# Products of softmax weights and values, per head in halves of TensorE's columns, in a kernel of block-sparse attention and a gated feed-forward block

## The chip, the cores and the metric

The kernel runs on one core of a Trainium2 chip. The metric is device time in microseconds (us): the median of three runs, 801.23 before the change (798.42 to 802.46). The engines of the core work side by side, each with its own queue of instructions: TensorE (PE; its weight loads are shown as PEld), VectorE (DVE), ScalarE (ACT), GpSimd (POOL), and SyncE (SP), which only issues DMAs.

## The reference

Four batches, eight heads of 64, 768 positions in 24 blocks of 32. A block of queries attends to itself and its two neighbours, to the first and last block, and to three sampled blocks; the first and last block attend to everything. A gated feed-forward block follows.

```python
scores = scale * np.matmul(q, k.transpose(0, 1, 3, 2))
mask = np.abs(blk_i - blk_j) <= window
mask = mask | (blk_i == 0) | (blk_j == 0) | (blk_i == n_blocks - 1) | (blk_j == n_blocks - 1)
...
scores = np.where(mask, scores, -1000000000.0)
scores = scores - np.max(scores, axis=-1, keepdims=True)
attn = np.exp(scores)
attn = attn / (np.sum(attn, axis=-1, keepdims=True) + 1e-09)
return np.matmul(attn, v).astype(np.float32)
...
g = x @ w_gate
silu = g * (1.0 / (1.0 + np.exp(-g)))
val = x @ w_val
return (silu * val @ w_out).astype(np.float32)
```

## The kernel before

**Numbers in two parts.** In batches 1 to 3 and in most of the feed-forward part an f32 number is held as two f16 numbers, high and low, and a product of two such numbers is three f16 products: high with high, high with low, low with high. Batch 0's attention is computed in f32 by functions of its own (`pair0`, `full_rows0`).

**Chunks.** The queries of each batch are taken in groups of 128 (four blocks); the chunks that the feed-forward part works on have two such groups in batch 0 (three chunks) and three in batches 1 to 3 (six chunks). For each chunk attention writes the tile `xall`, and then come 24 pieces of the first feed-forward product (`p`, L1693, 12 matmuls of 384 columns each) and 12 pieces of the second (`po`, L1756, 9 matmuls of 512 columns each). A chunk's feed-forward part begins when all of its attention is written; the norm `xn` (L1637) is part of that beginning.

**One block of queries, batches 1 to 3 (`block`).** VectorE copies the keys of the eight visible blocks into a ring of three slots (`kring`, L1114 and L1115), and DMAs bring the values to a ring of three (`w2all`: window by SyncE, L1121, the sampled blocks by GpSimd's indirect DMA, L1124). Two blocks form a pair: their scores (`qk`, L1137) are one task on PE of 32 matmuls, each in a quarter of PE's columns. Then VectorE takes the maxima (L1151), ScalarE the exponentials (L1168), the weights are split into high (ScalarE, L391) and low (VectorE, L394), and SyncE issues a transposing DMA that puts keys on the partitions (`pts`, L1193). Then comes the product with the values (`pv`, L1206): for each of four pairs of heads 6 matmuls of 64 columns, all 128 rows and 128 columns of PE wide. Both heads' values are the stationary operand (128 columns) and both heads' weights the moving one (64 columns), so that half of what is computed, one head's values with the other head's weights, isn't used. When two blocks have their products, `x_high` (ScalarE, L1227) and `x_low` (VectorE, L1232) write the high and the low part to `xall`, each with one instruction for each half of the partitions, because the two heads of a pair lie in different columns.

The rows of the first and the last block (`full_rows`) have scores `qkf` (L922) and products `pvf` (L991) in halves of PE's columns: one head's output in partitions 0 to 63, the other's in 64 to 127. Their products already hold the high and the low weights side by side as one moving operand.

**What sets the order.** The whole program is a list of tasks, each with an engine, a planned duration, the tasks that it needs, the ring buffers that it takes, and a rank. `Plan.order` runs through planned time. Whenever an engine is free, it takes the task of lowest rank among those that are ready and have their buffers. Ranks are a base (10 for each chunk of attention, 1000 more for its feed-forward part) plus an entry of the table `SHIFT`, which reaches from about -8700 to 6200. A task becomes ready 0.16 us (`SEM_US`) after the last task that it needs has ended. `in_turn` makes each task of a kind need the one before it of that kind; products of blocks and of full rows are of one kind, `"pv"`, scores of both are of one kind, `"qk"`. The pieces of the feed-forward part need each other in the same way. The order in which each engine's instructions are then issued is this planned order; on the chip every engine keeps to it.

The loads of a batch's keys and values (`load_kv`) go through SyncE's queue, in order with the transposing DMAs of attention.

Of the kernel before, what the change touches and what calls it, by code (L numbers as in the profile page):

```python
# [18 lines left out]
BLK = 32  # L19
# [22 lines left out]
DMA_US = 1.6  # L42
SEM_US = 0.16
# [61 lines left out]
class Task:  # L105
    __slots__ = ("eng", "us", "emit", "need", "rank", "take", "dma", "left", "outs", "next", "ready", "end", "no", "key", "late", "many")
# [13 lines left out]
class Plan:  # L120
# [9 lines left out]
    def add(self, eng, us, emit, need=(), rank=0.0, take=(), use=(), dma=None, behind=None, late=0.0, many=1):  # L130
        t = Task()
        t.late, t.many = late, many if dma is not None and eng != "POOL" else 0
# [31 lines left out]
    def order(self):  # L164
# [9 lines left out]
        done = []  # L174
        now = 0.0
        while len(done) < len(self.tasks):
            later = []
            moved = False
            for eng, list_ in waiting.items():
# [4 lines left out]
                for t in list_:  # L184
                    if t.ready > now:
                        later.append(t.ready)
                        continue
                    if best is not None and (t.rank, t.no) > (best.rank, best.no):
                        continue
# [8 lines left out]
                    best = t  # L198
# [6 lines left out]
                free[eng] = now + t.us  # L205
                t.end = now + t.us + t.late
                if t.dma is not None:
                    queue = max(max(queue, now + min(0.4, t.us)) + t.dma, t.end)
                    t.end = queue + DMA_US
                    for _ in range(t.many):  # L210
                        lanes.append(max(lanes.pop(0), t.end))
# [16 lines left out]
def tile_block_sparse_attn_swiglu(  # L228
# [657 lines left out]
    def full_rows(b, ci, sub, o, rank):  # L886
# [23 lines left out]
        for j in range(4):  # L910
# [43 lines left out]
            s = in_turn("qk", "PE", 0.87, scores, [o.done] + bt.k_done, rank, take=qk, use=[o.qs, bt.ks])  # L954
# [27 lines left out]
            def product(j=j, turned=turned):  # L982
                if j == 0:
                    get(pv, f"pvf_{b}")
                for c6 in range(6):
# [3 lines left out]
                    for l, w in ((0, P), (1, D)):  # L989
                        for hh in range(2):  # L990
# [8 lines left out]
            pvs.append(in_turn("pv", "PE", 0.68, product, there + vl, rank, take=[] if j else [pv],  # L999
                               use=turned + vbuf + ([pv] if j else [])))  # L1000
# [50 lines left out]
    def attention(ci, rank, qtiles):  # L1051
        b = CHUNKS[ci][0] // NTB
        bt = batches[b]
        for sub, si in enumerate(CHUNKS[ci]):
# [27 lines left out]
            for n in range(0, len(sparse), 2):  # L1082
                r = r0 + 0.05 * n
                if not b:
# [4 lines left out]
                       for i in range(2)]  # L1089
                first = [next(x) for x in two]  # L1090
                qks = [x[2] for x in first]
                a = in_turn("qk", "PE", 1.0, lambda first=first: [x[1]() for x in first], [x[0] for x in first] + [o.done], r,
                            take=qks, use=[o.qs])
# [4 lines left out]
    def block(ci, b, bt, o, sub, n, qb, col, rank, tsc, pv):  # L1098
# [96 lines left out]
        def product():  # L1195
# [3 lines left out]
            pvv = pv.tile.rearrange("p (j b q) -> p j b q", j=4, b=2)  # L1199

            for j in range(4):
                g, u = divmod(2 * j, 4)
                i = 0
                for cc in range(2):
                    for l, m in ((0, 0), (0, 1), (1, 0)):
                        nc.tensor.matmul(  # L1206
                            pvv[:, j, n % 2],
                            vg[:, cc, l, 2 * j : 2 * j + 2, :],
                            pq[:, g, m, cc, u : u + 2, :],
                            start=i == 0,  # L1210
                            stop=i == 5,
                        )
                        i += 1
# [3 lines left out]
        def x_views(hh):  # L1217
            hs_ = slice(hh * D, (hh + 1) * D)
            pvv = pv.tile.rearrange("p (j b q) -> p j b q", j=4, b=2)
            src = pvv[hs_, :, :, hh * BLK : (hh + 1) * BLK]  # L1220
            xt = xts[ci].tile
            return [src] + [xt[hs_, l, :, cols].rearrange("p j (b q) -> p j b q", b=2) for l in range(2)]

        def x_high():
            for hh in range(2):
                src, hi, _ = x_views(hh)
                nc.scalar.copy(hi, src)  # L1227

        def x_low():
            for hh in range(2):  # L1230
                src, hi, lo = x_views(hh)
                nc.vector.tensor_tensor(lo, src, hi, op=ALU.subtract)  # L1232
# [14 lines left out]
        a = in_turn("pv", "PE", 0.71, product, [a, vl, vi], rank, take=[pv] if n % 2 == 0 else [], use=[pts] + ([pv] if n % 2 else []))  # L1247
# [607 lines left out]
```

## Time and profile before

| | |
|---|---|
| median of three runs | 801.23 us (798.42 to 802.46) |
| the profiled execution | 800.0 us |
| its span, first to last instruction | 798.2 us |
| granted TensorE clock, mean of the span | 0.989 |
| products `pv`, L1206 | 1584 matmuls, busy 57.0 us |
| scores `qk`, L1137 | 1056 matmuls, busy 35.7 us |
| feed-forward `p`, L1693 | 2016 matmuls, busy 326.8 us |
| feed-forward `po`, L1756 | 900 matmuls, busy 195.3 us |

All of this is of one profiled execution. The views used below are: the page's busy times; busy time of each engine by stretches of the span; PE's timeline, in which consecutive matmuls of one line are one row with its start, its length from the first start to the last modelled end, and their count; groups of instructions by line and shape (after the bars: busy us, mean ns of one, and idle time before them); and waits. Matmuls overlap, so that rows of PE's timeline do too: the time that a group takes is read from its start to the next group's start.

### The profile page before, as it was taken

What the parts mean: (1) busy time and instruction counts of PE and PEld (TensorE: products, weight loads), DVE (VectorE), ACT (ScalarE), POOL (GpSimd) and SP (SyncE); (2) the same over time, 40 slices, a digit from 0 to 9 for tenths busy, and PEclk for the clock granted to TensorE, in tenths of its full rate; (3) what the DMA queues carried; (4) which work ended last, traced back from release to release, by engine and by line L of the source; (5) the groups of instructions that cost most, each with busy time, mean ns of one, the idle gap of its engine ahead of it and who ended that gap; (6) DMA issues with size and microseconds to landing.
All of it is one profiled execution on the core that took longest, in us unless ns stands there. A gap on an engine that the chain in (4) does not pass through costs nothing.

```text
span 798.2 us, 21196 instructions
## 1 busy us (share of the span) xinstructions
PE 762.4 (96%) x8098; PEld 489.2 (61%) x8098; DVE 547.4 (69%) x1658; ACT 504.5 (63%) x1211; POOL 205.7 (26%) x257
## 2 busy tenths in 40 slices
PE   3789999999999999999999999999999999999998
PEld 2557778884587566645665566645665566555655
DVE  5676898998898787742799866753798767731220
ACT  2687767587688686763598856754487757641221
POOL 3553511322033223201223222401223233101210
PEclk9889999999999999999999999999999999999999
DMA  8963537647877979478769994947878974330001
GB/s 205 259 220 118 193 146 260 205 125 230 198 151 172 212 169 197 91 197 265 159 134 182 269 227 114 203 97 211 188 133 179 228 177 105 69 69 19 1 1 39
DMA packets 171430, 128.08 MB, mean 160 GB/s; under 512 B 115008, under 2 KB 136896, under 8 KB 171328
## 3 DMA queue, kind: packets, MB, share of 16 engines
q1 hardware_dynamic: 165696, 109.42, 56.6%
q0 software_dynamic: 5632, 17.31, 8.5%
q8 instruction: 63, 1.03, 0.5%
q14 instruction: 39, 0.32, 0.1%
HBM read 79.50 MB, written 11.01 MB: 113 GB/s over the span
## 4 chain that ended last, share of the span: by engine, by line
PE 63%; DVE 18%; DMA 8%; issue 4%; ACT 4%; SPq 1%; DVEq 1%; ACTq 0%
PE p L1693 29%; PE po L1756 18%; PE pv L1206 4%; PE p L1687 3%; DMA q<-in_q_dram 3%; PE qk L1137 3%; DVE pp L394 2%; DVE act L1702 1%; DVE act L1707 1%; DMA pts<-pp 1%; DVE w1t L394 1%; DVE e L1151 1%; DMA stage<-in_k_dram 1%; DVE kring L1114 1%; PE qk L1341 1%
## 5 line engine op out<-in xcount | busy, mean ns | idle before, releaser
L1693 PE MATMUL p<-xall,w1t 128*128 128x384 f16 (+1 forms) x2016 | 326.8, 319 | 0.0
L1693 PEld LDWEIGHTS <-w1t 128*128 128x128 f16 x2016 | 191.2, 98 | 115.5 <-issue 8.5
L1715 POOL TENSOR_TENSOR h<-act,h 128x384 f16<-128x384 f32 (+1 forms) x108 | 101.6, 941 | 372.5 <-ACT h L1712 372.1
L1756 PE MATMUL po<-w2all,h 128*128 128x512 f16 (+1 forms) x900 | 195.3, 371 | 0.3 <-DVE w2all L394 0.3
L1756 PEld LDWEIGHTS <-h 128*128 128x128 f16 x900 | 84.6, 98 | 93.7 <-issue 5.6
L1712 ACT CAST h<-act 128x384 f16<-128x384 f32 (+1 forms) x108 | 50.8, 471 | 82.5 <-DVE act L1707 82.2
L1124 POOL DMA_INDIRECT w2all<-vd,vidx x66 | 62.8, 951 | 150.2 <-PE pv L1206 126.7
L1702 DVE SCALAR_TENSOR_TENSOR act<-act,p 128x384 f32<-128x384 f32 (+1 forms) x108 | 54.2, 504 | 65.2 <-ACT act L1698 64.5
L1687 PE MATMUL p<-xall,w1t 128*128 128x256 f32 x384 | 88.8, 384 | 0.4 <-DVE act L1702 0.3
L1168 ACT ACTIVATE e<-e,nb,es 128x256 f32<-128x256 f32 x132 | 78.2, 593 | 2.2
L1687 PEld LDWEIGHTS p<-xall,w1t 128*128 128x128 f32 x384 | 71.4, 192 | 12.0 <-DVE w2all L394 1.4
L1698 ACT ACTIVATE act<-p,gsc 128x384 f32<-128x384 f32 (+1 forms) x84 | 47.0, 560 | 31.2 <-PE p L1693 30.6
L1707 DVE SCALAR_TENSOR_TENSOR act<-act,hs,p 128x384 f32<-128x384 f32 (+1 forms) x84 | 49.7, 591 | 21.8 <-PE p L1693 18.8
L1206 PEld LDWEIGHTS <-w2all 128*128 128x128 f16 x1584 | 55.1, 98 | 13.9 <-issue 3.8
L394 DVE SCALAR_TENSOR_TENSOR pp<-e,rr,pp 128x256 f16<-128x256 f32 x132 | 61.2, 510 | 1.3 <-ACT pp L391 1.0
L391 ACT ACTIVATE pp<-e,rr 128x256 f16<-128x256 f32 x132 | 58.1, 496 | 3.7 <-DVE rr L782 2.5
L1206 PE MATMUL pv<-pts,w2all 128*128 128x64 f16 x1584 | 57.0, 193 | 2.8 <-DMA pts<-pp 2.8
L1151 DVE CUSTOM_DVE_ANT_1 e<-qk,msk 128x256 f32<-128x256 f32 x132 | 50.0, 417 | 2.8 <-issue 2.4
L1593 ACT ACTIVATE ot<-po,oc 128x512 f32<-128x512 f32 (+1 forms) x25 | 16.7, 667 | 42.9 <-PE po L1756 42.7
L1114 DVE COPY kring<-kst 128x256 f16 x198 | 38.9, 251 | 5.6 <-PE qk L1137 5.3
L1232 DVE TENSOR_TENSOR xall<-pv,xall 64x256 f16<-64x256 f32 x66 | 27.7, 420 | 21.1 <-ACT xall L1227 18.7
L1137 PE MATMUL qk<-kring,qs 128*32 128x256 f16 x1056 | 35.7, 274 | 0.2 <-DVE mx L1151 0.2
(187 smaller groups left out, 899.4 us busy)
## 6 DMA issues: line engine op xcount, KB each, us to landing
stage<-in_w_dram SPq DMA_DIRECT2D x36, 512.0 KB
w2all<-vd SPq DMA_DIRECT2D x66, 192.0 KB
qs<-qraw SPq DMA_DIRECT2D x72, 128.0 KB
out_dram<-ot SPq DMA_DIRECT2D x19, 256.0 KB
qn<-in_q_dram SPq DMA_DIRECT2D x36, 128.0 KB
qraw<-in_q_dram SPq DMA_DIRECT2D x36, 128.0 KB
stage<-in_v_dram SPq DMA_DIRECT2D x9, 512.0 KB
vd<-stage SPq DMA_DIRECT2D x9, 512.0 KB
```

What stands on the lines that cost most here:

```text
L391: nc.scalar.activation(hi, src, AF.Copy, scale=scale)
L394: nc.vector.scalar_tensor_tensor(lo, src, scale, hi, op0=ALU.mult, op1=ALU.subtract)
L1124: nc.gpsimd.indirect_dma_start(vf[0:96, 1, :], None, bt.vd, bass.IndirectOffsetOnAxis(ap=vidx[0:96, qb : qb + 1], axis=0))
L1137: nc.tensor.matmul(stv[u * BLK : (u + 1) * BLK, g].rearrange("p s k -> p (s k)"), o.q[:, l, h // 2, h % 2, col : col + BLK], kg[:, h].rear ...
L1151: nc.vector.tensor_tensor_reduce(ev[:, g], stv[:, g], o.g.msk[:, qb, :].unsqueeze(2).broadcast_to([P, 8, BLK]), scale=1.0, scalar=-3.0e38, ...
L1168: nc.scalar.activation(ev[:, g], ev[:, g], AF.Exp, bias=nb_[:, g : g + 1], scale=o.g.es[:, 0:1], accum_out=c["rs"][:, g : g + 1],)
L1206: nc.tensor.matmul(pvv[:, j, n % 2], vg[:, cc, l, 2 * j : 2 * j + 2, :], pq[:, g, m, cc, u : u + 2, :], start=i == 0, stop=i == 5,)
L1687: nc.tensor.matmul(t[:, 0:tc_], w[:, i + 1, k_ * P : (k_ + 1) * P], x_k(k_), start=k_ == 0, stop=k_ == NKT - 1)
L1693: nc.tensor.matmul(t[:, 0:tc_], w_[:, f, m, k_, :], x_k(k_, l), start=i == 0, stop=i == 11)
L1702: nc.vector.scalar_tensor_tensor(a_, a_, 1.0, pg.tile[:, 0:tc_], op0=ALU.add, op1=ALU.mult)
L1715: nc.gpsimd.tensor_tensor(hv(f)[:, 1, :], act.tile[:, 0:tc_], hv(f)[:, 0, :], op=ALU.subtract)
L1756: nc.tensor.matmul(po.tile[:, cs], hv(f)[:, l, ts_], w2h[:, f, m, cs], start=f == 0 and i == 0, stop=f == NF - 1 and i == 2)
```

## The change

The product of a block is made per head. The head's values are the stationary operand (64 columns), the output goes to its own half of the partitions, so that PE works in halves of its columns, and the two heads of a pair alternate. The head's high values meet its high and low weights side by side as one moving operand of 64 columns (high in the first 32, low in the second); its low values meet the high weights, 32 columns, added to the first half. So there are 32 matmuls for a block instead of 24. In the output the two halves of 64 columns must now be added: `x_high` rounds the first half to the high part, one instruction over all partitions, and `x_low` subtracts that from the first half and then adds the second half, two instructions over all partitions.

The planner gets a mark `thin` for the tasks in which PE works in parts of its columns (scores and products of blocks and of full rows in batches 1 to 3), a price of 0.097 us for PE's change between such tasks and others, and a rule: after a thin task, PE takes a ready thin task before any other, whatever the ranks. (`HOLD_US` holds only for tasks marked 2, of which there is none.) The planned durations of the thin tasks and of `x_high` and `x_low` are new. The table `SHIFT` stays as it is.

```diff
+TURN_US = 0.097
+HOLD_US = 6.0
...
-    def add(self, eng, us, emit, need=(), rank=0.0, take=(), use=(), dma=None, behind=None, late=0.0, many=1):
+    def add(self, eng, us, emit, need=(), rank=0.0, take=(), use=(), dma=None, behind=None, late=0.0, many=1, thin=False):
         t = Task()
+        t.thin = thin
...
+        thin = False
...
-                    if t.ready > now:
-                        later.append(t.ready)
+                    at = t.ready + (HOLD_US if t.thin == 2 and not thin else 0.0)
+                    if at > now:
+                        later.append(at)
                         continue
-                    if best is not None and (t.rank, t.no) > (best.rank, best.no):
+                    key = (eng == "PE" and thin and not t.thin, t.rank, t.no)
+                    if best is not None and key > low:
                         continue
...
-                    best = t
+                    best, low = t, key
...
-                free[eng] = now + t.us
-                t.end = now + t.us + t.late
+                us = t.us
+                if eng == "PE":
+                    us += TURN_US if bool(t.thin) != thin else 0.0
+                    thin = bool(t.thin)
+                free[eng] = now + us
+                t.end = now + us + t.late
...
-            s = in_turn("qk", "PE", 0.87, scores, [o.done] + bt.k_done, rank, take=qk, use=[o.qs, bt.ks])
+            s = in_turn("qk", "PE", 0.66, scores, [o.done] + bt.k_done, rank, take=qk, use=[o.qs, bt.ks], thin=True)
...
-            pvs.append(in_turn("pv", "PE", 0.68, product, there + vl, rank, take=[] if j else [pv],
-                               use=turned + vbuf + ([pv] if j else [])))
+            pvs.append(in_turn("pv", "PE", 0.54, product, there + vl, rank, take=[] if j else [pv],
+                               use=turned + vbuf + ([pv] if j else []), thin=True))
...
-                a = in_turn("qk", "PE", 1.0, lambda first=first: [x[1]() for x in first], [x[0] for x in first] + [o.done], r,
-                            take=qks, use=[o.qs])
+                a = in_turn("qk", "PE", 0.87, lambda first=first: [x[1]() for x in first], [x[0] for x in first] + [o.done], r,
+                            take=qks, use=[o.qs], thin=True)
...
-            pvv = pv.tile.rearrange("p (j b q) -> p j b q", j=4, b=2)
+            out_ = pv.tile.rearrange("p (j b lq) -> p j b lq", j=4, b=2)
 
             for j in range(4):
-                g, u = divmod(2 * j, 4)
-                i = 0
                 for cc in range(2):
-                    for l, m in ((0, 0), (0, 1), (1, 0)):
-                        nc.tensor.matmul(
-                            pvv[:, j, n % 2],
-                            vg[:, cc, l, 2 * j : 2 * j + 2, :],
-                            pq[:, g, m, cc, u : u + 2, :],
-                            start=i == 0,
-                            stop=i == 5,
-                        )
-                        i += 1
+                    for l, w in ((0, 2), (1, 1)):
+                        for hh in range(2):
+                            g, u = divmod(2 * j + hh, 4)
+                            nc.tensor.matmul(
+                                out_[hh * D : (hh + 1) * D, j, n % 2, 0 : w * BLK],
+                                vg[:, cc, l, 2 * j + hh, :],
+                                pq[:, g, 0:w, cc, u, :],
+                                start=cc == 0 and l == 0,
+                                stop=cc == 1 and l == 1,
+                            )
...
-        def x_views(hh):
-            hs_ = slice(hh * D, (hh + 1) * D)
-            pvv = pv.tile.rearrange("p (j b q) -> p j b q", j=4, b=2)
-            src = pvv[hs_, :, :, hh * BLK : (hh + 1) * BLK]
+        def x_views():
+            pvv = pv.tile.rearrange("p (j b l q) -> p j b l q", j=4, b=2, l=2)
             xt = xts[ci].tile
-            return [src] + [xt[hs_, l, :, cols].rearrange("p j (b q) -> p j b q", b=2) for l in range(2)]
+            return [pvv[:, :, :, i, :] for i in range(2)] + [xt[:, l, :, cols].rearrange("p j (b q) -> p j b q", b=2) for l in range(2)]
 
         def x_high():
-            for hh in range(2):
-                src, hi, _ = x_views(hh)
-                nc.scalar.copy(hi, src)
+            src, _, hi, _ = x_views()
+            nc.scalar.copy(hi, src)
 
         def x_low():
-            for hh in range(2):
-                src, hi, lo = x_views(hh)
-                nc.vector.tensor_tensor(lo, src, hi, op=ALU.subtract)
+            src, more, hi, lo = x_views()
+            nc.vector.tensor_tensor(lo, src, hi, op=ALU.subtract)
+            nc.vector.tensor_tensor(lo, more, lo, op=ALU.add)
...
-        a = in_turn("pv", "PE", 0.71, product, [a, vl, vi], rank, take=[pv] if n % 2 == 0 else [], use=[pts] + ([pv] if n % 2 else []))
+        a = in_turn("pv", "PE", 0.47, product, [a, vl, vi], rank, take=[pv] if n % 2 == 0 else [], use=[pts] + ([pv] if n % 2 else []), thin=True)
...
-            a = add("ACT", 0.76, x_high, [a, x_open(ci, rank)], rank, use=[pv, xts[ci]])
-            x_done[ci].append(add("DVE", 0.87, x_low, [a], rank, use=[pv, xts[ci]]))
+            a = add("ACT", 0.42, x_high, [a, x_open(ci, rank)], rank, use=[pv, xts[ci]])
+            x_done[ci].append(add("DVE", 0.88, x_low, [a], rank, use=[pv, xts[ci]]))
```

More of the change, by code (lines that the diff above doesn't have):

```diff
@@ L105 @@
 class Task:
-    __slots__ = ("eng", "us", "emit", "need", "rank", "take", "dma", "left", "outs", "next", "ready", "end", "no", "key", "late", "many")
+    __slots__ = ("eng", "us", "emit", "need", "rank", "take", "dma", "left", "outs", "next", "ready", "end", "no", "key", "late", "many", "thin")
 class Buf:
@@ L204, in order @@
                     self.given[b.ring].append(b)
-                free[eng] = now + t.us
-                t.end = now + t.us + t.late
+                us = t.us
[4 more added lines that the diff above has]
+                t.end = now + us + t.late
                 if t.dma is not None:
-                    queue = max(max(queue, now + min(0.4, t.us)) + t.dma, t.end)
+                    queue = max(max(queue, now + min(0.4, us)) + t.dma, t.end)
                     t.end = queue + DMA_US
```

## The prediction

> **What bounds the kernel now.** I read the page first: engine shares.
>
> ```profile
> span 798.2 us, 21196 instructions
> PE 762.4 (96%) x8098; PEld 489.2 (61%) x8098; DVE 547.4 (69%) x1658; ACT 504.5 (63%) x1211; POOL 205.7 (26%) x257
> ```
>
> TensorE (PE) is busy for 96% of the span. An average hides stages, so the second view is the busy time by stretches, cut at the places where the feed-forward part of a chunk begins (460, 547, 636) and where attention ends (712). Columns after the stretch: its length, then busy time of PE, weight loads, VectorE (DVE), ScalarE (ACT), GpSimd (POOL), granted clock, DMA share, GB/s.
>
> ```profile
> core 0: us, PE busy (x) PEld busy (x) DVE busy (x) ACT busy (x) POOL busy (x), PEclk, DMA share, GB/s
> 0.00:205.00 205.00, 177.54 (x2230) 133.21 (x2231) 164.93 (x382) 141.95 (x329) 69.21 (x110) 0.96 0.66 196
> 205.00:396.00 191.00, 187.69 (x1973) 120.10 (x1971) 136.58 (x461) 129.68 (x313) 45.31 (x51) 1.00 0.78 181
> 396.00:460.00 64.00, 63.23 (x792) 38.01 (x791) 57.03 (x220) 54.59 (x143) 18.46 (x19) 1.00 0.88 194
> 460.00:547.00 87.00, 87.00 (x864) 51.00 (x862) 51.40 (x160) 50.68 (x126) 20.65 (x22) 1.00 0.76 168
> 547.00:636.00 89.00, 87.95 (x937) 52.80 (x939) 69.06 (x245) 62.60 (x156) 23.04 (x24) 1.00 0.82 181
> 636.00:712.00 76.00, 76.00 (x819) 45.91 (x808) 52.19 (x162) 45.95 (x116) 18.01 (x19) 1.00 0.54 117
> 712.00:798.00 86.00, 83.00 (x507) 48.16 (x503) 16.23 (x33) 19.03 (x33) 10.96 (x12) 1.00 0.05 16
> ```
>
> The change works in batches 1 to 3, whose attention lies between 205 and 712 us. PE idles there for 3.31 + 0.77 + 0 + 1.05 + 0 = 5.1 us of 507. Up to 205 nothing changes (batch 0 has products of its own), and from 712 on only feed-forward work is left. So a microsecond less of PE work between 205 and 712 is a microsecond of time, but only while PE has other work to go on with. In 396 to 460 VectorE is busy for 57.03 of 64 us and DMA is at 0.88: there attention has limits of its own. That decides the case, so I looked at the borders of the chunks, in the timeline of PE (start, length, line, operation, count).
>
> ```profile
> 455.66 4.06 PE L1756 MATMUL po<-w2all,h 128*128 128x512 f16 x18
> 459.56 0.81 PE L1637 MATMUL xn<-sqx,ones_h 128*128 128x384 bf16 x4
> ...
> 543.25 4.05 PE L1756 MATMUL po<-w2all,h 128*128 128x512 f16 x18
> 547.13 2.11 PE L1693 MATMUL p<-xall,w1t 128*128 128x384 f16 x12
> ...
> 635.44 1.06 PE L1137 MATMUL qk<-kring,qs 128*32 128x256 f16 x32
> 636.43 2.12 PE L1693 MATMUL p<-xall,w1t 128*128 128x384 f16 x12
> ```
>
> At 459.56, 547.13 and 636.43 the last output products (po) of a chunk are followed at once by the first work of the next (xn or p), which needs that chunk's finished attention. At these three places PE has no stock of feed-forward work left.
>
> **The product itself.** The timeline of PE in a dense stretch:
>
> ```profile
> 432.65 2.11 PE L1756 MATMUL po<-w2all,h 128*128 128x512 f16 x9
> 434.69 1.06 PE L1137 MATMUL qk<-kring,qs 128*32 128x256 f16 x32
> 435.68 2.12 PE L1756 MATMUL po<-w2all,h 128*128 128x512 f16 x9
> ...
> 440.27 0.86 PE L1206 MATMUL pv<-pts,w2all 128*128 128x64 f16 x24
> 440.98 2.11 PE L1756 MATMUL po<-w2all,h 128*128 128x512 f16 x9
> 442.92 0.86 PE L1206 MATMUL pv<-pts,w2all 128*128 128x64 f16 x24
> ...
> 445.56 0.86 PE L1206 MATMUL pv<-pts,w2all 128*128 128x64 f16 x24
> ...
> 448.30 1.06 PE L1137 MATMUL qk<-kring,qs 128*32 128x256 f16 x32
> ```
>
> Lengths overlap, so I go from start to start. Nine full-width po matmuls of 512 columns take 442.92 - 440.98 = 1.94 us, 0.421 ns a column. The old product (pv, 24 matmuls) takes 440.98 - 440.27 = 0.70 us, 29 ns each, of which 27 are its 64 columns. The scores (qk) work in quarters of the array's columns. The po before them takes 434.69 - 432.65 = 2.04, so 0.10 goes on entering the narrow form. The scores then take 0.99, of which 8 rounds x 256 columns x 0.421 = 0.86 are streaming, so 0.13 goes on leaving it, small starts included. Narrow work that stands alone pays 0.23.
>
> For halves of the columns there is a near relative, the product of the full rows (pvf): 6 rounds of two pairs, one of 128 and one of 64 columns.
>
> ```profile
> 327.27 0.71 PE L991 MATMUL pvf<-ptsf,stage 128*64 128x128 f16 x24
> 327.91 2.12 PE L1693 MATMUL p<-xall,w1t 128*128 128x384 f16 x12
> ```
>
> It takes 0.64. Two halves one after the other would stream 2304 columns, 0.97 us; side by side 1152, 0.49. So they do run side by side.
>
> The new product has 32 matmuls in 16 pairs: 8 pairs of 64 columns (high values, against high and low weights side by side) and 8 of 32 (low values). Of the 66 blocks each issues 8 matmuls and 8 weight loads more. What a pair of 32 costs no row shows. By streaming alone the body is 768 columns x 0.421 = 0.32. The weight loads speak for more (mean ns is the number before the last bar):
>
> ```profile
> L1206 PEld LDWEIGHTS <-w2all 128*128 128x128 f16 x1584 | 55.1, 98 | 13.9 <-issue 3.8
> L1137 PEld LDWEIGHTS <-qs 128*32 128x32 f16 x1056 | 25.2, 96 | 11.9 <-issue 7.1 <-DVE mx L1151 1.0 <-DVE act L1702 1.0
> L991 PEld LDWEIGHTS <-stage 128*64 128x64 f16 x288 | 6.9, 111 | 4.4 <-issue 4.4
> ```
>
> A load of 64 columns takes 111 - 96 = 15 ns longer than one of 32, so about 30 ns of a load of 64 columns are its columns (an estimate from these rows). A pair of 32, which streams 14 ns, doesn't cover the next load. I take 29 ns for every pair, as for the old matmul of 64 columns: 16 x 29 = 0.47, with 0.10 and 0.13 a product of 0.70 where it stands **alone**. Old 0.70, new 0.70: nothing. Bounds: 0.32 + 0.23 = 0.55 (66 x -0.15 = -9.9 us); and, if each matmul with its load costs pvf's 0.64 / 24 = 27 ns, 32 x 27 + 0.10 = 0.95 (66 x +0.25 = +16.5 us).
>
> The Trainium skill speaks against the change: by "TensorEngine Tiling (Array Packing)", section "Gotcha 2: Feature Incompatibilities", column tiling rules out the fast weight load, and by "TensorE: Matmul & The Clock Gate", section "LDWEIGHTS (loading the stationary operand)", a load takes its columns / 1.2 GHz, 53 ns for 64. The first agrees with the rows (64 columns take 111 ns, 128 take 98). By the second a body would be 16 x 53 = 0.85 and the sum 66 x 0.38 = 25 us worse before anything is joined; but pvf's 12 pairs, with the leaving taken off, took (0.64 - 0.13) / 12 = 43 ns, which is less than 53 even with half of them streaming 128 columns.
>
> **Joining.** The gain is in narrow work that follows narrow work: one leaving and one entering, 0.23, go for each join. The new ordering takes narrow work first once PE is narrow. Two products can't be joined: a task in turn is ready 0.16 us after the one before it of its kind, and by then a feed-forward piece, long ready, is taken (the timeline shows exactly that now: pv, po, pv, po). So joins are of products with scores. There are 33 score tasks of the band and 12 of full rows. That scores often are ready early shows in VectorE's timeline:
>
> ```profile
> 439.44 0.42 DVE L1151 CUSTOM_DVE_ANT_1 e<-qk,msk 128x256 f32<-128x256 f32 x1
> ...
> 441.16 0.35 DVE L1115 COPY kring<-kst 128x768 f16<-128x768 f16 x1
> ```
>
> The keys of the scores that start at 448.30 were in place at 441.51, and the buffers of the scores before were read at 439.86: they could have followed the product at 442.92. I take 34 joins: about 27 band scores (the first two of each batch come before any product), a few of full rows, and a few with a product on either side. 34 x 0.23 = **-7.8 us**. Bounds: no join, 0; both sides of all 45 score tasks, 90 x 0.23 = -20.7.
>
> **Evacuation, and the order.** ScalarE's copy loses half its instructions, VectorE keeps its number:
>
> ```profile
> L1227 ACT CAST xall<-pv 64x256 f16<-64x256 f32 x66 | 24.0, 363 | 18.1 <-PE pv L1206 17.5
> L1468 ACT CAST xall<-pv 128x256 f16<-128x256 f32 x3 | 1.1, 370 | 0.0
> ...
> L1232 DVE TENSOR_TENSOR xall<-pv,xall 64x256 f16<-64x256 f32 x66 | 27.7, 420 | 21.1 <-ACT xall L1227 18.7 <-ACT h L1712 1.2 <-issue 0.5
> L1469 DVE TENSOR_TENSOR xall<-pv,xall 128x256 f16<-128x256 f32 x3 | 1.2, 414 | 0.0
> ```
>
> Twice the partitions cost the same (370 against 363, 414 against 420). ACT loses 66 x 0.363 - 33 x 0.370 = 11.7 us, VectorE nothing; its second operation now needs the first one's result. ACT isn't the bound anywhere, so I count 0; uncovered, at the three borders, it is 0.36 us each.
>
> The prices of scores and full rows issue nothing; they only move the planned order. No instruction waits for a new kind of thing. But what the joins save in 396 to 460 and 547 to 636, where VectorE is fullest and a border without stock ends the stretch, I count as lost: PE is early and waits. These hold 12 of the 66 products each, 24 / 66 x 7.8 = **+2.8 us**.
>
> Sum: 0 - 7.8 + 2.8 = -5.0. The profiled execution took 800.0 us (span 798.2 and 1.8 around it), 1.2 below the median of 801.2; so 795.0 there, and **796** for the median.
>
> **Rivals.**
> 1. *Given back in full.* Attention, not PE, sets each border, and an order made by ranks that belong to the old one puts some more waiting in. Against the 5.1 us idle now, 8 more take all of the 7.8: 801, between 799 and 804. For it: the three borders without stock. Against: PE waits almost nowhere for attention's products now:
>
> ```profile
> PE pv L1206 <- DMA pts<-pp: 2.8, 3, 1.3
> ```
>
> 2. *Short pairs only stream.* Then 0.55 a product: -9.9 - 7.8 = -17.7, of which 24 / 66 is lost again, -11.3, 790; between 786 and 792. Against it: the load row of 111 ns.
> 3. *Slower: late loads of the next batch.* SyncE's queue is in order, and its transposes wait there for VectorE (total, times, longest):
>
> ```profile
> SPq L1193 <- DVE pp L394: 54.8, 24, 10.9
> ```
>
> If in the new order the loads of keys and values of batches 2 and 3 come behind one more such wait, the stretch that ends without stock begins that much later. With the longest, 10.9 us, at one batch: -7.8 + 10.9 = +3.1, 804; at both +14, 815. It decides above 7.8 us in all; the mean wait, 54.8 / 24 = 2.3, doesn't reach it.
> 4. *Slower: weight loads bind.* 0.95 a product: +16.5 - 7.8 = +8.7, 810. By the 53 ns of the Trainium skill it would be 25 - 7.8 = +17.
>
> That the change doesn't do what it says (halves side by side) is as good as excluded by pvf's 0.64.
>
> **How the numbers follow.** Forecast 796 (792 to 800): 0.43. Rival 1: 0.25. Rival 2: 0.15. Rival 3: 0.12. Rival 4: 0.05. I call 0.5% (4 us) what a measurement can tell from no change: faster is below 797.2, slower above 805.2. Of the forecast's own range 0.30 lie below 797.2 and 0.13 above; with rival 2 faster is 0.45. Same is 0.13 + 0.25 = 0.38, and rivals 3 and 4 give slower, 0.17. The range 788 to 804 leaves out rivals 3 and 4 and the far end of rival 2.
>
> **What would show it.** In the new profile: a product that stands alone takes 0.60 from its start to the next full-width start, with 0.10 before it; PE busy between 205 and attention's end about 8 us less; some 34 places where scores and product adjoin with no full-width work between them; about 3 us more of PE idle, at the ends of the second and fourth stretch. A product's body near 0.32 is rival 2, near 0.85 rival 4. If first scores of a batch come later than the end of the attention before them explains, it is rival 3. The forecast is wrong if joins are few (under 15), or if new idle time of PE is over 6 us.

## The result: slower, and the profile after

| | median us | lowest to highest | ratio to before (95%) |
|---|---|---|---|
| before | 801.62 | 797.03 to 810.19 (20 runs) | |
| after | 810.13 | 802.28 to 817.77 (20 runs) | 1.0089 (1.0062 to 1.0115) |

The change makes the kernel 0.9% slower, about 7 us; 796 was forecast. The ratio leaves out runs more than 1.5% above their kernel's fastest (slow runs), the medians don't, and the profiled execution of after is one of those left out. It took 814.53 us (span 812.8), 4.4 above the median and 14.6 above the profiled execution of before, twice what the ratio says. So the account in this section is of that one execution; which of its idle places the order brings back in other executions stands under the experiments.

The page's busy times, the answer to the first fence of the prediction:

```profile
span 812.8 us, 22167 instructions
PE 766.2 (94%) x8626; PEld 480.3 (59%) x8626; DVE 548.3 (67%) x1658; ACT 489.2 (60%) x1178; POOL 205.5 (25%) x257
```

The busy times by stretches, cut at the same events as before (the columns are those of the prediction's second fence):

```profile
0.00:205.00 205.00, 178.03 (x2236) 133.76 (x2237) 165.81 (x384) 143.20 (x331) 68.43 (x110) 0.95 0.67 197
205.00:396.00 191.00, 184.38 (x2121) 114.96 (x2120) 134.72 (x449) 122.64 (x299) 45.45 (x51) 0.98 0.78 179
396.00:470.00 74.00, 70.56 (x926) 40.20 (x925) 63.29 (x240) 57.11 (x150) 19.93 (x20) 0.98 0.91 205
470.00:551.00 81.00, 76.39 (x888) 43.66 (x887) 50.38 (x148) 46.38 (x110) 20.54 (x22) 1.00 0.72 159
551.00:644.00 93.00, 91.73 (x1053) 52.38 (x1052) 72.11 (x268) 61.25 (x159) 22.73 (x24) 0.98 0.81 173
644.00:718.00 74.00, 73.61 (x882) 43.59 (x881) 46.72 (x143) 41.18 (x101) 17.48 (x19) 1.00 0.55 106
```

Between 205 and 718 TensorE (PE) now idles 6.62 + 3.44 + 4.61 + 1.27 + 0.39 = 16.3 us, where it was 5.1: **11.2 more**. The granted clock, 1.00 in all these stretches before, is 0.98 in three of them. PE's timeline shows the places, with the idle time before a row and what ended it in brackets:

```profile
267.52 1.06 PE L1147 MATMUL qk<-kring,qs 128*32 128x256 f16 x32
271.86 1.04 PE L1216 MATMUL pv<-pts,w2all 128*64 128x64 f16 x32 [3.28 <-DMA pts<-pp]
...
461.39 1.47 PE L1216 MATMUL pv<-pts,w2all 128*64 128x64 f16 x64
464.78 0.32 PE L1699 MATMUL p<-xall,w1t 128*128 128x384 f16 x1 [1.92 <-ACT xall L1233]
465.84 3.27 PE L1699 MATMUL p<-xall,w1t 128*128 128x384 f16 x11 [0.73 <-DVE xall L1238]
...
542.57 4.06 PE L1762 MATMUL po<-w2all,h 128*128 128x512 f16 x18
550.07 1.08 PE L1643 MATMUL xn<-sqx,ones_h 128*128 128x384 bf16 x4 [3.44 <-ACT sqx L1638]
550.94 1.49 PE L1762 MATMUL po<-w2all,h 128*128 128x512 f16 x3
```

At 271.86 a product, joined to the scores before it, waits 3.28 us for its transposed weights. At 464.78 a chunk's stock has run out: p waits 1.92 + 0.73 us for the attention of its own chunk. At 550.07 there still is stock (po follows at 550.94), but the norm xn stands in front of it in PE's queue and waits 3.44 us for ScalarE. The same three places in busy times (each pair of rows is the idle place and what follows it):

```profile
267.50:271.80 4.30, 1.07 (x40) 0.87 (x33) 3.96 (x16) 1.90 (x6) 0.92 (x1) 0.86 1.20 157
270.60:277.40 6.80, 5.54 (x43) 2.57 (x43) 3.60 (x17) 1.42 (x3) 1.17 (x1) 0.50 1.13 200
461.40:465.10 3.70, 1.67 (x66) 1.37 (x66) 2.06 (x7) 3.54 (x10) 1.84 (x2) 1.00 1.08 256
465.20:468.50 3.30, 2.66 (x9) 1.31 (x9) 0.55 (x2) 1.89 (x3) 0.00 (x0) 0.50 1.24 253
546.50:550.00 3.50, 0.12 (x1) 0.00 (x0) 0.00 (x0) 2.50 (x4) 0.00 (x0) 1.00 1.06 368
550.50:553.80 3.30, 3.30 (x10) 1.18 (x8) 1.34 (x7) 1.65 (x4) 0.00 (x0) 0.50 1.02 204
```

After each of the last two, and from 270.6 on within the first, the granted clock is 0.50. PE is busy there for 5.54 + 2.66 + 3.30 = 11.5 us at half speed, so **5.8 us** more are lost in this execution. (Over the 17 runs of after that the ratio compares, span x (1 - clock), the time lost to half clock, is 11.5 us a run on the mean; for the runs of before in the experiments it is 8.0 to 9.0. So half clock is about 3 of the 7 us, an estimate from these clocks.) Where the end moved to is seen behind the last xn, in PE's timeline of after:

```profile
717.07 0.81 PE L1643 MATMUL xn<-sqx,ones_h 128*128 128x384 bf16 x4
717.72 21.53 PE L1762 MATMUL po<-w2all,h 128*128 128x512 f16 x99
```

and at the same place of before:

```profile
716.21 0.81 PE L1637 MATMUL xn<-sqx,ones_h 128*128 128x384 bf16 x4
716.86 7.93 PE L1756 MATMUL po<-w2all,h 128*128 128x512 f16 x36
```

Attention ends at the same time, within 0.9 us, but 99 / 9 = 11 pieces of po are left where 36 / 9 = 4 were. Seven pieces of 1.95 us are 13.7, and with the 0.9 that is the difference of the spans, 812.8 - 798.2 = 14.6. The balance: 11.2 of idle and 5.8 of half clock make 17.0, so that narrow work itself must have become some 2.4 us shorter. That is seen in the single steps:

```profile
455.80 1.06 PE L1147 MATMUL qk<-kring,qs 128*32 128x256 f16 x32
456.79 0.68 PE L1216 MATMUL pv<-pts,w2all 128*64 128x64 f16 x32
457.40 4.06 PE L1762 MATMUL po<-w2all,h 128*128 128x512 f16 x18
...
505.28 0.68 PE L1216 MATMUL pv<-pts,w2all 128*64 128x64 f16 x32
505.81 0.82 PE L932 MATMUL qkf<-kst,qs 128*64 128x384 f16 x8
506.56 2.12 PE L1699 MATMUL p<-xall,w1t 128*128 128x384 f16 x12
508.61 0.68 PE L1216 MATMUL pv<-pts,w2all 128*64 128x64 f16 x32
509.23 2.12 PE L1699 MATMUL p<-xall,w1t 128*128 128x384 f16 x12
```

A product takes 0.61 to full-width work (457.40 - 456.79), and the p before one takes 508.61 - 506.56 = 2.05, 0.10 more than before full-width work: 0.71 alone, 0.70 was forecast. Scores before a product take 456.79 - 455.80 = 0.99, **the same as before full-width work** (435.68 - 434.69 in the prediction). Only where both are in halves of the columns is the leaving saved: the product before qkf takes 505.81 - 505.28 = 0.53. (The 64 matmuls at 461.39 are two products that adjoin because no feed-forward piece was left to stand between them; the prediction had said that two products can't be joined.)

The evacuation came out as priced (groups of after; 361 ns, and 416 and 424 ns, 33 times each):

```profile
L1233 ACT CAST xall<-pv 128x256 f16<-128x256 f32 x33 | 11.9, 361 | 8.5 <-PE pv L1216 8.4
...
L1238 DVE TENSOR_TENSOR xall<-pv,xall 128x256 f16<-128x256 f32 x33 | 14.0, 424 | 1.1
L1237 DVE TENSOR_TENSOR xall<-pv,xall 128x256 f16<-128x256 f32 x33 | 13.7, 416 | 7.8 <-ACT xall L1233 7.7
```

### The profile page after: what moved, and what is told of

It reads as the page before. It is cut to its first block, busy times and chain, and to the rows that moved or that the text cites. A ratio compares the mean times of both kernels' runs of the same rounds, so it can differ in the third digit from the quotient of the medians.

```text
span 812.8 us, 22167 instructions
## 1 busy us (share of the span) xinstructions
PE 766.2 (94%) x8626; PEld 480.3 (59%) x8626; DVE 548.3 (67%) x1658; ACT 489.2 (60%) x1178; POOL 205.5 (25%) x257
## 5 line engine op out<-in xcount | busy, mean ns | idle before, releaser
L1762 PEld LDWEIGHTS <-h 128*128 128x128 f16 x900 | 86.7, 99 | 97.4 <-issue 7.1
L404 DVE SCALAR_TENSOR_TENSOR pp<-e,rr,pp 128x256 f16<-128x256 f32 x132 | 68.0, 558 | 2.6 <-ACT pp L401 2.5
L401 ACT ACTIVATE pp<-e,rr 128x256 f16<-128x256 f32 x132 | 58.6, 496 | 10.3 <-DMA pts<-pp 5.7
L1216 PEld LDWEIGHTS <-w2all 128*64 128x64 f16 x2112 | 39.7, 113 | 25.7 <-issue 25.4
L1216 PE MATMUL pv<-pts,w2all 128*64 128x64 f16 (+1 forms) x2112 | 45.3, 191 | 5.6 <-DMA pts<-pp 4.3
L1124 DVE COPY kring<-kst 128x256 f16 x198 | 36.5, 242 | 2.1 <-PE qk L1147 1.9
L1147 PEld LDWEIGHTS <-qs 128*32 128x32 f16 x1056 | 24.9, 96 | 14.1 <-issue 8.2
```

Of the source, the lines that this page charges most:

```text
L401: nc.scalar.activation(hi, src, AF.Copy, scale=scale)
L404: nc.vector.scalar_tensor_tensor(lo, src, scale, hi, op0=ALU.mult, op1=ALU.subtract)
L1147: nc.tensor.matmul(stv[u * BLK : (u + 1) * BLK, g].rearrange("p s k -> p (s k)"), o.q[:, l, h // 2, h % 2, col : col + BLK], kg[:, h].rear ...
L1216: nc.tensor.matmul(out_[hh * D : (hh + 1) * D, j, n % 2, 0 : w * BLK], vg[:, cc, l, 2 * j + hh, :], pq[:, g, 0:w, cc, u, :], start=cc == 0 ...
L1762: nc.tensor.matmul(po.tile[:, cs], hv(f)[:, l, ts_], w2h[:, f, m, cs], start=f == 0 and i == 0, stop=f == NF - 1 and i == 2)
```

## The experiments

Theory A: the instructions are harmless, and the loss is in the order, because the table of ranks fits the old sequence of the planner's decisions and no other. Theory B: the new instructions cost by themselves. Theory C: what PE saves is given back at the borders of chunks whatever one does. Theory D: the rule or the prices are bad in themselves. Ratios are to before, measured on the same chip; each stands with its 95% interval.

### The new product in the old order, and the old product in the new order

The first takes the new `product`, `x_views`, `x_high` and `x_low` into the kernel before and leaves everything of the planner alone. The second does the reverse. The edit of the first, cut:

```diff
-                    for l, m in ((0, 0), (0, 1), (1, 0)):
+                    for l, w in ((0, 2), (1, 1)):
+                        for hh in range(2):
...
-            for hh in range(2):
-                src, hi, _ = x_views(hh)
-                nc.scalar.copy(hi, src)
+            src, _, hi, _ = x_views()
+            nc.scalar.copy(hi, src)
...
+            nc.vector.tensor_tensor(lo, more, lo, op=ALU.add)
```

> The new product, ScalarE's one copy and VectorE's two operations, in the order of the kernel before (its planner, prices and rule untouched). If the order is what costs (theory A), this is as fast as before: 66 products at 0.70 us where they stand alone, old 0.70, so a ratio of 1.000, between 0.996 and 1.003, and none of the new idle of TensorE (3.28 us before the product at 271.86, 2.65 at the p at 464.78, 3.44 at the xn at 550.07). If the new instructions cost by themselves (theory B: weight loads, the second operation of x_low), it is slower like the changed kernel: 1.006 or more.

> The old product and the old evacuation in the changed kernel's order. Theory A: the idle places of the changed kernel are here too, and the joins are worth less, since the old product is full width (a scores task beside it still enters and leaves the narrow form): 1.010 to 1.018. Theory B: about as before, 0.998 to 1.004.

Measured: the new product in the old order 803.23 us, 1.0011 (0.9980 to 1.0043); the old product in the new order 813.38 us, 1.0140 (1.0090 to 1.0189). Theory B falls and theory A stands. The instructions cost nothing that can be measured; the order alone costs 1.4% with the old product. With the new product it costs (1.0089 - 1.0011) x 801 = 6.2 us (2.9 to 9.5 with both intervals); whether the new product takes some of the 1.4% back isn't shown, the intervals overlap.

The second run has the changed kernel's order, and so has the run with fewer matmuls in the new order further below. Their PE timelines show which idle places come back; the first three rows are of the old product in the new order, the others of the run with fewer matmuls:

```profile
460.54 0.32 PE L1703 MATMUL p<-xall,w1t 128*128 128x384 f16 x1 [2.30 <-ACT xall L1237]
461.43 3.50 PE L1703 MATMUL p<-xall,w1t 128*128 128x384 f16 x11 [0.57 <-DVE xall L1242]
543.12 0.81 PE L1647 MATMUL xn<-sqx,ones_h 128*128 128x384 bf16 x4 [0.30 <-ACT sqx L1642]
...
459.44 0.32 PE L1699 MATMUL p<-xall,w1t 128*128 128x384 f16 x1 [2.69 <-ACT pp L401]
542.53 1.12 PE L1643 MATMUL xn<-sqx,ones_h 128*128 128x384 bf16 x4 [2.18 <-ACT sqx L1638]
```

The wait of p at the border of its chunk is in all three profiled executions with this order (1.92 + 0.73 us in after, 2.30 + 0.57 here, and 2.69 + 0.74 in the last) and not in before. The wait of xn varies: 3.44, 0.30 and 2.18. The product that waited 3.28 us at 271.86 doesn't wait in the second of these executions and waits 0.71 us in the third, so the order alone doesn't make that wait.

One execution's idle time is a rough measure. The profiled execution of the new product in the old order took 811.82 us, 8.6 above its median. It has neither the wait of p nor that of xn, but its products wait 7.6 us for transposed weights, and PE idles 523.01 - 510.49 = 12.5 us from 205 us to its last xn.

### Joins in the old order

The same as the first, with the narrow tasks pulled in front of one feed-forward piece where they were ready:

```diff
+def joined(plan, done):
...
+        for a, x, n in zip(pe, pe[1:], pe[2:]):
+            if not narrow(n) or not narrow(a) or narrow(x) or x.key[:1] not in ("p", "o"):
+                continue
...
+            if any(at[h] > at[x] or h.end + SEM_US > x.ready for h in held if h is not n):
+                continue
+            done.remove(n)
+            done.insert(at[x], n)
...
-    for t in plan.order():
+    for t in joined(plan, plan.order()):
         t.emit()
```

> As the first of these, with one thing more: in the order of before, a narrow task that stands one feed-forward piece behind another narrow task and was ready by the plan ahead of that piece is put in front of it. 24 joins in the plan, as the changed kernel has, and nothing else moved. If joining is worth 0.23 us each and costs nothing (theory A: only the reshuffling of everything else costs), 22 x 0.23 = 5 us less than the first: a ratio of 0.992 to 0.996. If narrow tasks pulled ahead wait for their transposed weights (theory C: the join itself makes PE wait, as at 271.86), 0.998 to 1.006, and the product waits for DMA by more than 5 us in all.

Measured: 802.83 us, 1.0019 (0.9990 to 1.0048). The expected gain of 5 us isn't there, and neither is theory C's wait: the products wait for DMA for 2.8 us in all, as before:

```profile
PE pv L1235 <- DMA pts<-pp: 2.8, 5, 1.2
```

So the joins happened, did no harm that can be measured, and were worth too little to be seen. Counted along PE's timeline, 24 tasks adjoin, most of them scores and product, for which 0.10 is saved and not 0.23.

### Joins of the right kind: products with products

```diff
+def paired(plan, done):
...
+        if not product(a) or not product(n) or x.key[:1] not in ("p", "o"):
+            continue
...
+        done.remove(x)
+        done.insert(at[a], x)
...
-    for t in plan.order():
+    for t in paired(plan, plan.order()):
         t.emit()
```

> The new product in the order of before, with one thing moved: where two products stand with one feed-forward piece between them and that piece could have run ahead of the first, it is put ahead, so that the two products adjoin (22 pairs in the plan; the first of them runs 1.95 us later, nothing waits more for its data). The traces so far show that a change between scores (quarters of the columns) and products (halves) costs as much as one to full width: 0.99 us for scores before a product as before full-width work, so that a join of the two saves the 0.10 of entering alone. Two products in halves should save both, 0.61 + 0.10 - 0.52 = 0.19 each. Theory A1 (the joins were of the wrong kind): 22 x 0.19 = 4.2 us below the new product in the old order, a ratio of 0.994 to 0.998 to before. Theory C (PE's time saved is given back at the borders of the chunks whatever the kind of join): 0.999 to 1.004.

Measured: 807.97 us, 1.0088 (1.0057 to 1.0119): slower than the same kernel without the move (1.0011), which neither theory expected. PE's timeline of this run shows the pair (64 matmuls in one row) and a later price of it:

```profile
444.62 1.19 PE L1232 MATMUL pv<-pts,w2all 128*64 128x64 f16 x64
445.74 4.06 PE L1778 MATMUL po<-w2all,h 128*128 128x512 f16 x18
449.73 0.68 PE L1232 MATMUL pv<-pts,w2all 128*64 128x64 f16 x32
453.28 1.04 PE L1232 MATMUL pv<-pts,w2all 128*64 128x64 f16 x32 [2.87 <-DMA pts<-pp]
454.25 4.02 PE L1778 MATMUL po<-w2all,h 128*128 128x512 f16 x9
```

A pair takes 445.74 - 444.62 = 1.12, and 1.22 with the entering of 0.10, where two apart take 2 x 0.71 = 1.42: the saving of 0.20 is real. But its waits row says that products now wait for DMA for 10.3 us in all:

```profile
PE pv L1232 <- DMA pts<-pp: 10.3, 9, 2.9
```

and the 9 matmuls of po behind the longest of these waits take 458.21 - 454.25 = 3.96 instead of 1.94, at half clock. Before has 2.8 us of such waits and the profiled execution without the move 7.6, so the row by itself doesn't show how many of the 10.3 come from the move. The first product of a pair ran 1.95 us later by the plan; that what followed from it on the other engines was late for later products is likely but not shown. Which of its followers (the release of the values' slot, of the transposed weights' buffer) it would be wasn't tried.

### The rule alone, the prices alone

```diff
-TURN_US = 0.097
+TURN_US = 0.0
...
-            s = in_turn("qk", "PE", 0.66, scores, [o.done] + bt.k_done, rank, take=qk, use=[o.qs, bt.ks], thin=True)
+            s = in_turn("qk", "PE", 0.87, scores, [o.done] + bt.k_done, rank, take=qk, use=[o.qs, bt.ks], thin=True)
```

and so on for the other planned durations: the rule alone. For the prices alone:

```diff
-                    key = (eng == "PE" and thin and not t.thin, t.rank, t.no)
+                    key = (False, t.rank, t.no)
...
-            a = add("ACT", 0.42, x_high, [a, x_open(ci, rank)], rank, use=[pv, xts[ci]])
+            a = add("ACT", 0.76, x_high, [a, x_open(ci, rank)], rank, use=[pv, xts[ci]])
```

> The new product and the rule that narrow work goes first after narrow work, with the planned durations of before and no price for a change of form. Theory A (the old ranks fit one order only, so any change of the planner's decisions costs): slower than before, 1.004 to 1.014, with new idle of TensorE at borders of chunks. Theory D (the rule is harmless and the new prices spoil the order): 0.996 to 1.002.

> The new product, the new prices of scores, full rows and products and the price of a change of form, without the rule (the planned durations of the evacuation are those of before). Theory A: slower than before although each price is closer to what the trace shows, 1.008 to 1.025. Theory D': the rule alone spoils the order, and this is 0.996 to 1.002.

Measured: the rule alone 811.17 us, 1.0134 (1.0088 to 1.0179); the prices alone 819.72 us, 1.0233 (1.0189 to 1.0277). The prices alone are slower than both together (1.0089); for the rule alone the intervals overlap. That each new price is closer to the trace, as the expectation has it, doesn't hold for the two most frequent tasks. Scores that stand alone cost 0.66 + 2 x 0.097 = 0.85 by the plan, where the trace has 0.99 + 0.10 = 1.09 and the old price was 0.87; a product costs 0.47 + 2 x 0.097 = 0.66, where the trace has 0.71 and the old price was 0.71. So this run doesn't separate worse prices from other decisions; the fitted table below does, with the same prices.

### What a microsecond of PE is worth

```diff
-                    for l, w in ((0, 2), (1, 1)):
+                    for l, w in ((0, 2),):
...
-                                stop=cc == 1 and l == 1,
+                                stop=cc == 1,
```

> What a microsecond of TensorE is worth in each order. The products' low values are left out (16 matmuls instead of 32, the output lacks those terms), in the order of before: by the trace a product then takes about 0.24 us less, 66 x 0.24 = 16 us of TensorE. If TensorE sets the time in this order (theory A), 11 to 16 us less than the new product in the old order: a ratio to before of 0.981 to 0.988. If attention's own chain sets it and TensorE's savings are given back at the borders (theory C), at most 5 us: 0.995 to 1.001.

> The same omission in the changed kernel's order: again 16 us of TensorE less. Theory A with stalls by order: there TensorE already waits at places where the work after it isn't ready, so less comes out, 6 to 11 us below the changed kernel: a ratio to before of 0.994 to 1.002. Theory C says the same 5 us or less as in the old order: 1.003 or more.

Measured: in the old order 794.32 us, 0.9939 (0.9909 to 0.9969); in the new order 804.13 us, 1.0043 (1.0012 to 1.0074). PE's timeline of the first:

```profile
432.52 0.44 PE L1206 MATMUL pv<-pts,w2all 128*64 128x64 f16 x16
432.89 2.12 PE L1752 MATMUL po<-w2all,h 128*128 128x512 f16 x9
```

A product takes 0.37 instead of 0.61, and 66 x 0.24 = 15.8 us of PE are gone. Of these, (1.0011 - 0.9939) x 801 = 5.8 us come out (2.3 to 9.3 with both intervals), a good third; in the new order (1.0089 - 1.0043) x 801 = 3.7 (0.4 to 7.0). In the old order that is less than theory A expected, and both sizes are near theory C's 5 us. Its place, the borders, isn't confirmed: in the profiled execution of the first PE idles 501.71 - 488.15 = 13.6 us from 205 us to its last xn, where before has 5.1, and the waits are spread, 5.9 us in 7 places for transposed weights and only 1.7 at xn. A PE that is busy for 96% of the span isn't the bound in the sense that its time is the kernel's time.

### Is it VectorE?

```diff
-            hi, lo, ev = views()
-            for g in range(2):
-                lo_part(lo[:, g], ev[:, g], c["rr"][:, g : g + 1], hi[:, g])
+            _, lo, _ = views()
+            nc.gpsimd.memset(lo, 0.0)
```

> Is VectorE what takes TensorE's savings back? The new product in the order of before, with the low weights left at zero: VectorE's two operations a block are left out (132 x 0.51 = 67 us of VectorE less) and GpSimd, which is busy for a quarter of the span, writes zeros in their place; the output lacks the terms with low weights, TensorE does the same work. If VectorE bounds the stretches whose chunks end without stock (theory V), 5 us or more below the new product in the old order: a ratio to before of 0.995 or less. If no single engine does and the order, each engine's queue and the waits between them hold the time (theory A), 0 to 2 us: 0.998 to 1.002.

Measured: 797.92 us, 0.9973 (0.9949 to 0.9997), 0.4% or 3 us below the new product in the old order (with both intervals from nothing to 6). VectorE is busy for 500.0 us, 44 less than in that kernel (543.8): the operations left out were busy for 61.1, less than the 67 expected, and other work on VectorE became longer. The ratio lies between the two expectations and nearer to theory A, but the interval doesn't exclude theory V's 5 us. VectorE's time, too, comes out only in small part, about 3 of 44 us. No run leaves out work of both engines, so whether PE's savings run into VectorE isn't settled.

### A table fitted to the new rules

The changed kernel with another table, and the new product under the old rules with another table; nothing else is edited. The entries were changed at random, and a change was kept where the planned order, with later DMAs and slower engines, still ended earlier.

```diff
-    "a0.0": 215.65, "a0.1": -2208.54, "a1.0": 2743.2, "a1.1": -905.98, "a2.0": -5449.96, "a2.1": 1137, "a3.0": -2069.74,
...
+    "a0.0": 6927.86, "a0.1": -2392.08, "a1.0": -120.69, "a1.1": 0.0, "a2.0": -7927.18, "a2.1": 2243.8, "a3.0": -4012.3,
...
```

> The changed kernel with the same instructions, prices and rule, and with the table of ranks fitted to them: changed at random and kept where the planned order, run through again with DMAs 0.6 us later or engines 3 to 4% slower, ends earlier. The planned end goes from 799.4 to 794.8 us, below the 796.3 of before; run through with those delays its mean goes from 811.4 to 804.7 (the order of before: 804.0). If it is the fit of the table to the order that was lost (theory A), this takes 5 to 8 us off the changed kernel: a ratio to before of 0.998 to 1.003. If the new rule and prices are bad whatever the table (theory D), 1.006 or more.

> The new product with the planner's rules and prices of before and a table fitted on in the same way, from the table of before (the mean of the delayed runs goes from 803.9 to 802.4 us). Theory A: 0 to 2 us below the new product in the old order, a ratio of 0.997 to 1.001; a version that beats before if its interval ends below 1.

Measured: the changed kernel with the fitted table 797.17 us, 1.0006 (0.9978 to 1.0033); the old rules with a fitted table 797.88 us, 1.0015 (0.9989 to 1.0042). The first takes the whole loss off, (1.0089 - 1.0006) x 801 = 6.6 us, with the same instructions, prices and rule. The planner's own figures point the same way without any run: in the expectation above the planned end of the changed order is 799.4 against 796.3 for the old one, and with the delays 811.4 against 804.0, 7.4 us apart where about 7 were measured. The prediction doesn't use them. The border at which p waited for its chunk reads, in this run's PE timeline:

```profile
454.75 2.12 PE L1761 MATMUL po<-w2all,h 128*128 128x512 f16 x9
456.70 2.11 PE L1698 MATMUL p<-xall,w1t 128*128 128x384 f16 x12
458.65 0.81 PE L1642 MATMUL xn<-sqx,ones_h 128*128 128x384 bf16 x4
459.30 2.11 PE L1698 MATMUL p<-xall,w1t 128*128 128x384 f16 x12
```

without a gap. From 205 us to its last xn at 703.6 this execution (797.12 us, at its median) has 498.60 - 490.97 = 7.6 us of idle PE, against 16.3 in the profiled execution of after, and its clock is at 1.00:

```profile
205.00:703.60 498.60, 490.97 (x5860) 291.54 (x5859) 359.33 (x1242) 328.93 (x815) 125.57 (x135) 1.00 0.78 172
```

Theory A is shown for the changed kernel: the same order costs with either product, the new product costs nothing without it, and another table under the same rule and prices takes the loss away. Theory D falls by the same run. But no version with the whole computation is measurably faster than before.

## Why the prediction was wrong

**Bounds.** That PE's idle time between 205 and 712 was small (5.1 us) and that three borders had no stock was read rightly. The conclusion, that a microsecond less of PE work is a microsecond of time while there is stock, was wrong in size: a third comes out (5.8 of 15.8 us). The step that took 24 / 66 of the savings as lost should have taken about two thirds; that VectorE is the reason isn't shown.

**The product.** Forecast 0.70 alone; 0.71 measured. Part of the closeness is luck: the body is 0.51 and not 0.47, and the leaving 0.10 and not 0.13. That a pair of 32 columns costs about as much as one of 64 holds: the run without the low values saves 0.24 us for 8 pairs of 32, 30 ns a pair, and the other 8 take 34 each (0.37 - 0.10 for the leaving, over 8). That the weight loads are the reason isn't shown. Rivals 2 and 4, the other prices, are excluded by these numbers.

**The joins: the step that failed first.** "One leaving and one entering, 0.23, go for each join" was taken for any two narrow tasks. Scores work in quarters and products in halves, and between them the full leaving is paid. No row of before shows such a change: the scores at 408.42 stand in front of a full-width product and those at 454.68 behind one. So the term needed a bound of its own below 0.23. Counted in after: 25 joins, 7 of halves with halves (0.19) and 18 of unlike forms (0.10), 3.1 us in place of 7.8; less 66 x 0.01 for the product that is about the 2.4 us that the balance above asks for. The Trainium skill has the rule, in "TensorEngine Tiling (Array Packing)", section "Key Properties": changing the tiling mode, as against the tile, drains TensorE. The trace agrees in the time: 0.99 us for scores before a product in halves as before full-width work.

**The order: the step that decided the sign.** The prediction counted a new order at nothing beyond the borders' share of 2.8, so that joins and order came to -5.0; measured, the changed order costs 6.2 us against the same instructions in the old one. An order with more waiting was left to rival 1 (8 us, 0.25), whose mechanism is the one that happened: new idle at the borders (2.65 us at 464.78, 3.44 at 550.07) and at a joined product (3.28 at 271.86), 11.2 us in all in the profiled execution, of which only the wait at 464.78 is in every profiled execution with this order. Two things were missing in its price. The three longest idle places are each followed or overlapped by some microseconds at half clock, 5.8 us in this execution and about 3 on the mean. And the table is fitted to the sequence of decisions: the rule alone costs 1.3%, the changed prices alone 2.3%, a table fitted to both takes the loss away. Rival 3 (late loads of the next batch) ends on the right side, but nothing here shows that loads caused the loss.

**What would show it**, as the prediction put it: product alone, yes; joins, 25 for 34; idle over 6 us, which was named as what would make the forecast wrong.

**Open** is which of the tasks that changed places leads to each of the three idle places, and what takes most of PE's savings back; that it is the coupling of the in-order queues is a guess from the pair experiment, not shown.

## What to carry to other kernels

Where the order comes from a planner with fitted ranks, a change of prices or of a rule can change the whole order and cost more than it saves: measure the instructions in the frozen old order first, then fit anew before judging the rule. The worth of an engine's microsecond is measured by leaving work out, not read from its busy share; here about a third came out at 96% busy. One profiled execution can lie 8.6 us from its kernel's median, as here, so its idle places need a second execution before they are put down to a change. A join of narrow matmuls saves the change of form only if both have the same form.

## What the runs showed of the hardware

Half clock can follow short idle. In after the granted clock was 0.50 for the 6.8 us from 270.6, when PE had stood idle for 2.0 us (from 268.58; the wait went on to 271.86), for 3.4 us from 465.1, after 1.92 us of idle, and for 3.4 us from 550.5, after 3.44. In the 3.41 us before these three drops PE was busy for 1.41, 1.35 and 0.40 us. Not every such wait is followed by a drop: in the new product in the old order PE was busy for 1.58 of the 4.10 us from 279.0, with a wait of 2.52, and the clock stayed at 1.00 there and behind it. The Trainium skill, "TensorE: Matmul & The Clock Gate", section "What's actually happening", has the drop after an idle window of about 3.4 us that runs freely; the lengths at half clock agree, but the drops at 270.6 and 465.1 came after 3.41 us in which PE was busy for about 40% of the time.

Two products in halves behind one another take 1.12 us, and one takes 0.61 to full-width work: so 1.12 - 0.61 = 0.51 is the product and 0.10 the leaving; the entering is the 0.10 more that the piece before a product takes.
